# Attention probabilities transposed by a DMA through DRAM instead of on TensorE (top-k attention followed by a gated feed-forward block)

## The chip, the cores and the metric

The kernel runs on one core of a Trainium2 chip. The metric is device time in microseconds (us), the median of several runs. Profiles are taken of one execution each; their own time is given beside their span.

## The reference

The inputs q, k and v have the shape (batch 8, heads 8, sequence 576, head width 64); the weights are w_in (512 x 2048) and w_out (2048 x 512). All arithmetic is in float32.

```python
scores = (q @ k.T) / 8                      # per batch and head, 576 x 576
kth    = 32nd largest of each row
scores = where(scores >= kth, scores, -1e9)
attn   = softmax(scores)                    # divided by (sum + 1e-9)
x      = (attn @ v), heads side by side     # 4608 tokens x 512
h      = x @ w_in                           # 4608 x 2048
out    = (h * cos(h)) @ w_out               # 4608 x 512
```

## The kernel before

**Units.** The attention work is cut into 144 units: 128 rows of queries times one pair of heads. One unit's scores are a tile `s` of 128 partitions x 2 heads x 576 keys. The main loop has one iteration, called a slot here, per unit. It is written out by hand, and each engine carries out its instructions in the order in which the loop issues them. In slot i four units are in work: `u` (unit i) has its 32 largest scores per row found on VectorE; `w` (unit i-1) is masked and exponentiated on ScalarE, gets its reciprocal on VectorE and is normalised on GpSimd; `x` (unit i-2) is transposed; `y` (unit i-3) is multiplied with v on TensorE. The scores of unit i+1 are also made in slot i.

**What each engine is given in a slot, in order.**
- VectorE (DVE): four rounds of `topk_round(u, 0..3)` (two `max` and two `match_replace` in each, the last round only the two `max`). `reciprocal(w)` (a `tensor_scalar` on `den`, then the reciprocal) stands between round 2 and round 3; it waits for ScalarE's exponentials of w.
- ScalarE (ACT): evictions of feed-forward results (`take_banks`), `take_values(y)`, `take_scores` of unit i+1, then `mask(w)` and `exponentials(w)`, which need the bounds of w, then `take_transposes(x)` (three copies out of PSUM) and the sines of the feed-forward part.
- GpSimd (POOL): `bounds(w)` (two tiny instructions that need the last round of w), `gate` (one product of 128 x 1024), `reduce_first` and `reduce_second` (three `tensor_scalar` and one `tensor_tensor` of 128 x 1024 for the range reduction of the cosine, in those slots that have a finished tile of h), then `normalise(w)` (two `tensor_scalar` of 128 x 576).
- TensorE (PE): `values(y)`, the scores of unit i+1, two feed-forward units, `transposes(x)` (nine transposes of 128 x 128 against an identity), and the remaining feed-forward units.
- SyncE (SP) issues all DMAs in program order: loads of q, k, v and of the weights, and stores of the output.

**The feed-forward part** is fed into the gaps of TensorE in units of eight matmuls of 128 x 256 on the profile's count (`ff1`, first product) or four of 128 x 512 (`ff2`, second product), 288 of each. A credit of 3.7 units per slot, capped at 5, limits the feeding. What is left when the units run out is done by a loop at the end, in which VectorE takes over the work that GpSimd had.

**The first eight units** (`EARLY`) are treated differently, because the weights are decoded at that time on ScalarE, VectorE and GpSimd: for them the transposition, the product with v and its eviction all lie in the same slot as the exponentials, and GpSimd has `normalise(w)` before the decoding (`decode_third`, pairs of `tensor_tensor`) and before `reduce_first` and `reduce_second`.

PSUM has a tile with the tag `sc` in one copy, used by the scores and by the transposes in turn, and one with the tag `ot`, used by the values and by the last transpose.

Of the kernel before, what the change touches and what calls it, by code (L numbers as in the profile page):

```python
# [10 lines left out]
F32 = mybir.dt.float32  # L11
I32 = mybir.dt.int32
U32 = mybir.dt.uint32
AF = mybir.ActivationFunctionType
ALU = mybir.AluOpType

P = 128
# [13 lines left out]
def kernel(  # L31
# [9 lines left out]
    nc = tc.nc  # L41
    ctx.enter_context(tc.manual_schedule())
    B, H, D, S = qT.shape
    DM, DF = moe_w_in.shape
    NT = S // P
    TAIL = S - NT * P
    MAIN = NT * P
# [9 lines left out]
    work = ctx.enter_context(tc.tile_pool(name="work", bufs=2))  # L57
    small = ctx.enter_context(tc.tile_pool(name="small", bufs=4))
    ps = ctx.enter_context(tc.tile_pool(name="ps", bufs=2, space=bass.MemoryType.PSUM))
    ffw = ctx.enter_context(tc.tile_pool(name="ffw", bufs=2))  # L60

    ident = consts.tile([P, P], F32, tag="ident")
# [10 lines left out]
    words = 2 if DECODE else 1  # L73
# [7 lines left out]
    for i in range(DF // CW):  # L81
        w = consts.tile([P, NC, CW], F32, tag=f"w_in{i}", name=f"w_in{i}")
# [4 lines left out]
    for f in range(NF):  # L87
        w = consts.tile([P, DM], F32, tag=f"w_out{f}", name=f"w_out{f}")
# [3 lines left out]
    ff = {"live": 0, "tick": 0, "now": 0, "credit": 0.0, "end": False, "kind": 0}  # L92
# [21 lines left out]
    def decode_first(n):  # L114


        for _ in range(min(n, len(wq["loaded"]))):
            st, w = wq["loaded"].popleft()
            lo, hi = st[:, :, 0], st[:, :, 1]
            nc.scalar.activation(out=w, in_=hi.bitcast(F32), func=AF.Abs, scale=2.0**16)  # L120
            nc.scalar.sign(hi.bitcast(F32), hi)
            nc.scalar.mul(out=lo, in_=lo.bitcast(U32), mul=2.0**-29)
            wq["second"].append((st, w))
# [79 lines left out]
                    )  # L203

    def take_scores(u):
        s = u["s"] = work.tile([P, 2, S], F32, tag="s", name="s", bufs=4)
        nc.scalar.copy(  # L207
            out=s.rearrange("p j (h w) -> p (j h) w", h=2),
            in_=u.pop("sc").rearrange("p j h w -> p (j h) w")[:, :, 0:HS],
        )  # L210

    def topk_round(u, rnd):
        s = u["s"]
        if rnd == 0:
            u["m8"] = small.tile([P, 2, TOPK], F32, tag="m8", name="m8")
            u["rest"] = work.tile([P, 2, S], F32, tag="rest", name="rest", bufs=1)
        m8, rest = u["m8"], u["rest"]
        src = s if rnd == 0 else rest
        at = slice(8 * rnd, 8 * rnd + 8)
        for j in range(2):  # L220
            nc.vector.max(m8[:, j, at], src[:, j])  # L221
        if rnd < TOPK // 8 - 1:
            for j in range(2):
                nc.vector.match_replace(rest[:, j], m8[:, j, at], src[:, j], NEG)  # L224
        else:
            del u["rest"]
# [12 lines left out]
    def mask(u):  # L239

        s, nb = u["s"], u.pop("nb")
        for j in range(2):
            nc.scalar.activation(  # L243
                out=s[:, j], in_=s[:, j], func=AF.Prelu, bias=nb[:, j, 1:2], scale=SCALE, alpha=FAR
            )

    def exponentials(u):
        s, nd = u["s"], u.pop("nd")
        den = u["den"] = small.tile([P, 2], F32, tag="den", name="den")
        for j in range(2):  # L250
            nc.scalar.activation(  # L251
                out=s[:, j], in_=s[:, j], func=AF.Exp, bias=nd[:, j : j + 1], scale=1.0,
                accum_out=den[:, j : j + 1],
            )

    def reciprocal(u):
        den = u.pop("den")
        nc.vector.tensor_scalar(out=den, in0=den, scalar1=EPS, scalar2=None, op0=ALU.add)
        u["rden"] = small.tile([P, 2], F32, tag="rden", name="rden")
        nc.vector.reciprocal(u["rden"], den)  # L260

    def normalise(u):
        s, rden = u["s"], u.pop("rden")
        for j in range(2):
            nc.gpsimd.tensor_scalar(  # L265
                out=s[:, j], in0=s[:, j], scalar1=rden[:, j : j + 1], scalar2=1.0,
                op0=ALU.mult, op1=ALU.mult,
            )

    def transposes(u):  # L270

        s = u.pop("s")
        tp = u["tp"] = ps.tile([P, 2, 2, 512], F32, tag="sc", name="tp", bufs=1)
        for j in range(2):
            for c in range(NT):
                k0 = j * TAIL + c * P
                nc.tensor.transpose(  # L277
                    tp[:, 0, j, c * P : (c + 1) * P], s[:, j, k0 : k0 + P], ident
                )
        tt = u["tt"] = ps.tile([P, 512], F32, tag="ot", name="tt", bufs=1)  # L280
        nc.tensor.transpose(
            tt[:, 0:P], s.rearrange("p j k -> p (j k)")[:, MAIN : MAIN + P], ident
        )

    def take_transposes(u):
        tp, tt = u.pop("tp"), u.pop("tt")
        pT = u["pT"] = work.tile([P, 2, NT * P], F32, tag="pT", name="pT")
        for j in range(2):
            nc.scalar.copy(out=pT[:, j], in_=tp[:, 0, j])  # L289
        pt = u["pT_tail"] = work.tile([P, P], F32, tag="pT_tail", name="pT_tail")  # L290
        nc.scalar.copy(out=pt, in_=tt[:, 0:P])  # L291

    def values(u):

        pT, pt = u.pop("pT"), u.pop("pT_tail")
        o = u["o"] = ps.tile([P, 512], F32, tag="ot", name="o", bufs=1)
        for b, _, rows, r0 in u["parts"]:
            st = pairs[b, u["hp"]]
            r = slice(r0, r0 + rows)
            for c in range(NT + 1):  # L300
                for j in range(2):
                    d = slice(j * D, (j + 1) * D)
                    if c < NT:
                        lhsT, rhs = st["v"][:, c, d], pT[:, j, c * P + r0 : c * P + r0 + rows]
                    else:
                        lhsT, rhs = st["v_tail"][:, d], pt[:, r]
                    nc.tensor.matmul(o[d, r], lhsT, rhs, start=c == 0, stop=c == NT)  # L307

    def take_values(u):
# [95 lines left out]
    def sines(least):  # L405
# [4 lines left out]
        for _ in range(n):  # L410
            blk, g, x, _, scale = waiting.popleft()
            nc.scalar.activation(out=x, in_=x, func=AF.Sin, bias=halfpi, scale=scale)  # L412
            sined.append((blk, g, x))

    def gate(n):
        for _ in range(min(n, len(sined))):
            blk, g, x = sined.popleft()
            eng = nc.vector if ff["end"] else nc.gpsimd
            eng.tensor_tensor(out=g, in0=g, in1=x, op=ALU.mult)  # L419
            blk["gated"].append(ff["tick"])  # L420
# [42 lines left out]
    def feed(n):  # L463

        ff["tick"] += 1
        while n > 0 and ff["credit"] >= 1:
            for kind in (ff["kind"], 1 - ff["kind"]):
                if (can_first, can_second)[kind]():
                    break
            else:  # L470
                return
            if kind == 0:
                ff1(*first.popleft())
            else:
                ff2(*second.popleft())
            ff["kind"] = 1 - kind
            n, ff["credit"] = n - 1, ff["credit"] - 1
# [30 lines left out]
    for i in range(NU + 3):  # L508
        ff["end"] = i >= NU
        u, w, x, y = (units[i - n] if 0 <= i - n < NU else None for n in range(4))  # L510
        early = w and i - 1 < EARLY
        if x and i - 2 < EARLY:
            x = None
        if y and i - 3 < EARLY:
            y = None
        ff["credit"] = min(ff["credit"] + 3.7, 5.0)
        ff["now"] += 1
        wq["ready"] = wq["done"]
        if w:
            bounds(w)  # L520
        if u:
            if i > 0:
                decode_second()
            topk_round(u, 0)
        take_banks()
        if y:
            values(y)
        if i + 1 < NU:
            scores(units[i + 1])
        if y:  # L530
            take_values(y)
        if i + 1 < NU:
            take_scores(units[i + 1])
        for load, b, hp in at_slot.get(i, []):
            load(b, hp)
        gate(1)
        if w:
            mask(w)
            exponentials(w)
        if early:  # L540
            reciprocal(w)
            normalise(w)
        if u:
            topk_round(u, 1)
            topk_round(u, 2)
        if w and not early:
            reciprocal(w)
        feed(2)
        take_banks()
        if i > 0:  # L550
            decode_third()
            decode_first(3)
        load_weights(3)
        reduce_first()
        if x:
            transposes(x)
            take_transposes(x)
        feed(4)
        if early:
            transposes(w)  # L560
            take_transposes(w)
            values(w)
            take_values(w)
        reduce_second()
        if w and not early:
            normalise(w)
        if u:
            topk_round(u, 3)
        sines(2)
# [47 lines left out]
```

## Time and profile before

| | |
|---|---|
| median of 3 runs | 1696.09 us (1695.43 to 1697.95) |
| the profiled execution | 1698.95 us, its span 1697.0 us |
| PE busy | 1559.6 us (92%) |
| DVE busy | 1523.7 us (90%) |
| ACT busy | 1165.5 us (69%) |
| POOL busy | 844.8 us (50%) |
| DMA queue of the loads and stores | 54.54 MB, 10.4% of 16 engines |
| transposes on PE (L277, L281) | 1296 matmuls, 197.1 us busy, overlapping |
| their evictions on ACT (L289, L291) | 432 copies, 193.2 us busy, overlapping |

Busy times of one engine overlap, since instructions are pipelined; where the time of a piece of work counts, the distance from its start to the start of what follows is the better measure. "L277" is line 277 of the kernel before. An entry "A <- B" among the waits says that A stood idle until B was done. The line numbers of the changed kernel are shifted: by 2 up to `normalise` and by some 15 after the new functions.

### The profile page before, as it was taken

Reading aid. Unit: us, or ns where it says so; the run is one execution under the profiler, and the core shown is the slowest. Engines: PE = TensorE matmul, PEld = TensorE weight load, DVE = VectorE, ACT = ScalarE, POOL = GpSimd, SP = SyncE. Lnnn points to the kernel's source line nnn. Section 1 sums busy time; section 2 is a strip of 40 time slices with the busy share of each in tenths; the row PEclk is TensorE's granted clock in tenths of the full one; section 3 lists DMA queues with packets and bytes.
Section 4 is the critical chain, followed back from the end, with each engine's and each line's share of the span. In section 5 each row is a group of like instructions: output and inputs, shape, how many; then the busy total and the mean of one; then the engine's idle time right before and its main releaser. Section 6 shows DMA issues by size and latency. Waiting matters only on the chain.

```text
span 1697.0 us, 26520 instructions
## 1 busy us (share of the span) xinstructions
PE 1559.6 (92%) x9616; PEld 1074.2 (63%) x9616; DVE 1523.7 (90%) x3261; ACT 1165.5 (69%) x2046; POOL 844.8 (50%) x968
## 2 busy tenths in 40 slices
PE   4556799797989999999999999999999999999998
PEld 2454577484766666666666666666666676666674
DVE  7999999999999999999999999999999999995220
ACT  6677567667576777777777777877777777776110
POOL 3678645455365555555545555555555554552000
PEclk9677899999999999999999999999999999999999
DMA  7332011001100021002000020011000110000000
GB/s 232 100 96 75 7 49 36 20 1 49 42 8 7 7 64 35 7 10 64 26 7 7 21 58 26 7 35 49 21 7 7 47 30 7 7 8 7 13 7 19
DMA packets 44227, 56.24 MB, mean 33 GB/s; under 512 B 10816, under 2 KB 27200, under 8 KB 44096
## 3 DMA queue, kind: packets, MB, share of 16 engines
q1 hardware_dynamic: 44096, 54.54, 10.4%
q8 instruction: 76, 1.25, 0.3%
q14 instruction: 55, 0.45, 0.1%
HBM read 45.09 MB, written 9.44 MB: 32 GB/s over the span
## 4 chain that ended last, share of the span: by engine, by line
PE 59%; ACT 16%; POOL 11%; DVE 11%; issue 2%; DMA 1%; SPq 0%; POOLq 0%; ACTq 0%
PE o L431 20%; PE mm L355 19%; PE o L307 8%; PE sc L197 8%; DVE m L221 5%; ACT s L251 5%; DVE rest L224 4%; PE tp L277 4%; ACT s L243 3%; POOL x L402 3%; ACT s L207 2%; POOL s L265 2%; ACT L251 2%; ACT pT L289 1%; POOL x L393 1%
## 5 line engine op out<-in xcount | busy, mean ns | idle before, releaser
L221 DVE MAX8 m<-rest 128x8 f32<-128x576 f32 x864 | 608.1, 746 | 0.0
L431 PE MATMUL o<-w_out,g 128*128 128x512 f32 x1152 | 548.5, 603 | 10.1 <-POOL g L419 7.0
L355 PE MATMUL mm<-xT,w_in 128*128 128x256 f32 (+1 forms) x2688 | 552.7, 353 | 0.3 <-ACT g L367 0.3
L355 PEld LDWEIGHTS mm<-xT,w_in 128*128 128x128 f32 x2688 | 446.9, 191 | 128.4 <-issue 89.8
L265 POOL TENSOR_SCALAR s<-s,rden 128x576 f32<-128x576 f32 x288 | 213.4, 753 | 441.6 <-DVE rden L260 289.5
L224 DVE MATCH_REPLACE8 rest<-m,rest 128x576 f32<-128x576 f32 x576 | 423.5, 743 | 0.0
L431 PEld LDWEIGHTS o<-w_out,g 128*128 128x128 f32 x1152 | 208.4, 191 | 197.5 <-issue 175.9
L207 ACT COPY s<-sc 128x1152 f32<-128x1152 f32 x144 | 161.2, 1120 | 127.4 <-PE sc L197 127.2
L243 ACT ACTIVATE s<-s,nb 128x576 f32<-128x576 f32 x288 | 207.6, 770 | 49.5 <-POOL nb L231 49.5
L251 ACT ACTIVATE s<-s,nd 128x576 f32<-128x576 f32 x288 | 219.9, 765 | 0.7
L307 PE MATMUL o<-pT,v 128*64 128x128 f32 (+1 forms) x2560 | 168.5, 277 | 55.8 <-ACT pT_tail L291 55.7
L307 PEld LDWEIGHTS o<-pT,v 128*64 128x64 f32 x2560 | 133.3, 142 | 133.9 <-ACT pT_tail L291 90.0
L224 DVE MATCH_REPLACE8 rest<-m,s 128x576 f32<-128x576 f32 x288 | 211.7, 743 | 0.0
L221 DVE MAX8 m<-s 128x8 f32<-128x576 f32 x288 | 202.1, 743 | 8.0 <-ACT s L207 8.0
L277 PE MATMUL tp<-ident,s 128*128 128x128 f32 x1152 | 156.7, 281 | 55.7 <-POOL s L265 45.6
L197 PE MATMUL sc<-k,q 64*128 64x288 f32 (+1 forms) x1280 | 193.1, 449 | 11.6 <-DMA k<-in_k_dram 11.6
L277 PEld LDWEIGHTS tp<-ident,s 128*128 128x128 f32 x1152 | 138.2, 145 | 102.3 <-POOL s L265 52.6
L393 POOL TENSOR_SCALAR x<-g 128x1024 f32<-128x1024 f32 x63 | 66.2, 1050 | 205.8 <-ACT g L367 205.8
L289 ACT COPY pT<-tp 128x512 f32<-128x512 f32 x288 | 152.8, 582 | 17.4 <-PE tp L277 15.7
L314 ACT COPY xT<-o 128x128 f32<-128x128 f32 x144 | 37.9, 263 | 182.1 <-PE o L307 182.0
L419 POOL TENSOR_TENSOR g<-g,x 128x1024 f32<-128x1024 f32 x62 | 146.9, 2369 | 11.6 <-ACT x L412 11.6
L402 POOL TENSOR_TENSOR x<-g,x 128x1024 f32<-128x1024 f32 x63 | 149.3, 2370 | 5.3
(44 smaller groups left out, 1254.4 us busy)
## 6 DMA issues: line engine op xcount, KB each, us to landing
q<-in_q_dram SPq DMA_DIRECT2D x32, 288.0 KB, 3.1
out_dram<-ob SPq DMA_DIRECT2D x36, 256.0 KB, 2.0
st<-in_moe_w_in_dram SPq DMA_DIRECT2D x16, 512.0 KB, 5.1
v<-in_v_dram SPq DMA_DIRECT2D x32, 256.0 KB, 3.0
st<-in_moe_w_out_dram SPq DMA_DIRECT2D x16, 512.0 KB, 3.5
k<-in_k_dram SPq DMA_DIRECT2D x32, 144.0 KB, 3.3
k<-in_k_dram SPq DMA_DIRECT2D x32, 128.0 KB, 3.3
v_tail<-in_v_dram SPq DMA_DIRECT2D x64, 16.0 KB, 2.7
```

What stands on the lines that cost most here:

```text
L197: nc.tensor.matmul(sc[r0 : r0 + rows, j, h, 0:HS], st["q"][d, q0 : q0 + rows], st["k"][d, h * HS : (h + 1) * HS], start=True, stop=True,)
L207: nc.scalar.copy(out=s.rearrange("p j (h w) -> p (j h) w", h=2), in_=u.pop("sc").rearrange("p j h w -> p (j h) w")[:, :, 0:HS],)
L221: nc.vector.max(m8[:, j, at], src[:, j])
L224: nc.vector.match_replace(rest[:, j], m8[:, j, at], src[:, j], NEG)
L243: nc.scalar.activation(out=s[:, j], in_=s[:, j], func=AF.Prelu, bias=nb[:, j, 1:2], scale=SCALE, alpha=FAR)
L251: nc.scalar.activation(out=s[:, j], in_=s[:, j], func=AF.Exp, bias=nd[:, j : j + 1], scale=1.0, accum_out=den[:, j : j + 1],)
L265: nc.gpsimd.tensor_scalar(out=s[:, j], in0=s[:, j], scalar1=rden[:, j : j + 1], scalar2=1.0, op0=ALU.mult, op1=ALU.mult,)
L277: nc.tensor.transpose(tp[:, 0, j, c * P : (c + 1) * P], s[:, j, k0 : k0 + P], ident)
L307: nc.tensor.matmul(o[d, r], lhsT, rhs, start=c == 0, stop=c == NT)
L355: nc.tensor.matmul(mm[:, at : at + w], w_in[f // FC][:, c, (f % FC) * P : (f % FC + 1) * P], blk["xT"][:, c], start=c == 0, stop=c == NC - 1,)
L402: nc.gpsimd.tensor_tensor(out=x, in0=g, in1=x, op=ALU.subtract)
L431: nc.tensor.matmul(o, g[:, at : at + P], w_out[f], start=f == 0, stop=f == NF - 1)
```

## The change

For all units behind the first eight, the nine transposes on TensorE and the three copies out of PSUM are replaced. GpSimd copies the normalised probabilities once more, with the low and the high 16-bit halves of each float32 put into two separate rows (`split`, 2304 elements of 16 bits per partition). SyncE stores these rows to a DRAM tile (576 KB), and in the next slot a DMA of the transposing kind reads them back as 256 rows of 1152 16-bit columns and writes them to `pT`, which gives each float32 word its two halves side by side again. `values` reads `pT` as before, in the same slot as before.

To get there in time, `reciprocal(w)` moves from behind round 2 to behind round 1 on VectorE, and `normalise(w)` with `split(w)` follows it directly; on GpSimd this puts both ahead of `reduce_first` and `reduce_second`, where `normalise` stood behind them. The tile `s` has three copies instead of four, the tag `sc` is no longer shared with transposes behind the first eight units, and the credit goes from 3.7 to 4.0 feed-forward units per slot. The first eight units keep their transposes on TensorE (`transposes_now`).

```diff
+    dram = ctx.enter_context(tc.tile_pool(name="dram", bufs=4, space=bass.MemoryType.DRAM))
...
     def take_scores(u):
-        s = u["s"] = work.tile([P, 2, S], F32, tag="s", name="s", bufs=4)
+        s = u["s"] = work.tile([P, 2, S], F32, tag="s", name="s", bufs=3)
...
+    def split(u):
+        s = u.pop("s").rearrange("p j k -> p (j k)").bitcast(U16)
+        halves = work.tile([P, 2, 2 * S], U16, tag="halves", name="halves", bufs=1)
+        nc.gpsimd.tensor_copy(out=halves, in_=s.rearrange("p (k h) -> p h k", h=2))
+        rows = u["rows"] = dram.tile([P, 2, 2 * S], U16, tag="rows", name="rows")
+        nc.sync.dma_start(out=rows, in_=halves)
+
     def transposes(u):
+        rows = u.pop("rows").rearrange("q h k -> (q h) k")
+        pT = u["pT"] = work.tile([P, 2 * NT + 1, P], F32, tag="pT", name="pT")
+        words = pT.rearrange("p c q -> p (c q)").bitcast(U16)
+        nc.sync.dma_start_transpose(
+            out=words.rearrange("p (c q) -> p c q", c=2 * NT + 1), in_=rows
+        )
-        s = u.pop("s")
-        tp = u["tp"] = ps.tile([P, 2, 2, 512], F32, tag="sc", name="tp", bufs=1)
...
-    def take_transposes(u):
...
-            nc.scalar.copy(out=pT[:, j], in_=tp[:, 0, j])
...
-        ff["credit"] = min(ff["credit"] + 3.7, 5.0)
+        ff["credit"] = min(ff["credit"] + 4.0, 5.0)
...
         for load, b, hp in at_slot.get(i, []):
             load(b, hp)
+        if x:
+            transposes(x)
         gate(1)
...
             topk_round(u, 1)
-            topk_round(u, 2)
         if w and not early:
             reciprocal(w)
+            normalise(w)
+            split(w)
+        if u:
+            topk_round(u, 2)
         feed(2)
...
         reduce_first()
-        if x:
-            transposes(x)
-            take_transposes(x)
         feed(4)
         if early:
-            transposes(w)
-            take_transposes(w)
+            transposes_now(w)
             values(w)
             take_values(w)
         reduce_second()
-        if w and not early:
-            normalise(w)
         if u:
             topk_round(u, 3)
```

## The prediction, made before the changed kernel had run

> **What bounds the kernel now.** I read the busy times by slice first, then busy times in windows, then the engines' timelines. From 600 us to 1550 us two engines are full at once:
>
> ```profile
> core 0: us, PE busy (x) PEld busy (x) DVE busy (x) ACT busy (x) POOL busy (x), PEclk, DMA share, GB/s
> 1200.00:1300.00 100.00, 98.07 (x574) 67.11 (x570) 98.73 (x219) 76.86 (x136) 54.98 (x64) 1.00 0.04 12
> 1550.00:1600.00 50.00, 50.00 (x210) 33.35 (x209) 11.94 (x12) 13.31 (x19) 0.76 (x1) 1.00 0.02 6
> ```
>
> In the first row PE and DVE are both above 98%; in the second, after the last unit, PE works off feed-forward units alone. The DVE timeline gives the length of a slot:
>
> ```profile
> 810.34 0.50 DVE L258 TENSOR_SCALAR den<-den 128x2 f32<-128x2 f32 x1
> ...
> 820.59 0.16 DVE L258 TENSOR_SCALAR den<-den 128x2 f32<-128x2 f32 x1
> ```
>
> The `den` before stood at 800.30, so slots last 10.04 and 10.25 us; I use 10.0. DVE needs that by itself: a `max` or `match_replace` follows the other after 0.66 us, 14 of them with their value loads are 9.6 us, the reciprocal 0.3. PE's order in one slot, from the chain that ended last:
>
> ```profile
> 815.35 1.92 PE mm L355 x8
> 817.27 1.72 PE o L431 x4
> 818.99 0.87 PE tp L277 x8
> 819.86 0.11 PE tt L281
> 819.97 1.73 PE mm L355 x8
> 821.70 1.72 PE o L431 x4
> 823.42 1.24 PE o L307 x20
> ```
>
> The transposes take 0.87 + 0.11 = 0.98 us, the values 1.24, scores 1.17, a feed-forward unit 1.73. With 3.7 units that is 9.8 us and a little for changes of kind. The place that will decide is the first stage, where GpSimd already has work between a normalise and the next bounds:
>
> ```profile
> 116.27 0.20 POOL L231 TENSOR_SCALAR nb<-m 128x4 f32<-128x4 f32 x1
> 116.55 0.19 POOL L236 TENSOR_TENSOR nd<-nb 128x2 f32<-128x2 f32 x1
> 120.07 1.47 POOL L265 TENSOR_SCALAR s<-s,rden 128x576 f32<-128x576 f32 x2 [3.32 <-ACT g L367]
> 121.50 1.29 POOL L139 TENSOR_TENSOR w_out<-w_out,st 128x512 int32<-128x512 int32 x1
> ...
> 139.41 1.47 POOL L265 TENSOR_SCALAR s<-s,rden 128x576 f32<-128x576 f32 x2 [3.31 <-ACT w_out L120]
> ```
>
> ```profile
> 119.49 0.17 DVE L258 TENSOR_SCALAR den<-den 128x2 f32<-128x2 f32 x1 [2.63 <-ACT s L251]
> ```
>
> Bounds at 116.27, next normalise at 120.07: 3.8 us in which POOL waits for mask, exponentials and reciprocal. Then 1.43 for the normalise, 8.1 for decoding, 6.0 for the range reduction, 3.8 again: 19.3 us, exactly the distance between the two normalises. It is a ring (normalise, POOL's other work, bounds, exponentials, reciprocal, normalise), and it is longer than DVE's own work, so DVE stands 2.63 us at `den`. Later this ring is harmless, because the reduction lies between bounds and normalise, beside ScalarE's part.
>
> **The change, part by part.**
>
> *PE and the credit.* 0.98 us per slot goes. At 4.0 units PE has 1.24 + 1.17 + 4 x 1.73 + about 0.2 = 9.5 us, below DVE's 10.0, so PE alone allows the slot to stay at 10.0. By the two programs' instruction order 89 feed-forward units follow the last scores before, 57 after: 32 x 1.73 = 55 us less tail. That is the whole gain, since DVE's work is unchanged. The removed evictions (about 1.3 us of ACT per slot) free an engine that is 77% busy and off the path: nothing by itself. Cover: were PE the later one, each 0.1 us per slot would cost 14 us over 136 slots.
>
> *Order on GpSimd.* Normalise and split now precede the range reduction, so the reduction lies between them and the next slot's bounds: the ring of the first stage is back in each slot with a reduction. Its length: bounds to normalise 3.8, normalise 1.43, split C, reduction 5.76 (in the timeline the four instructions start at 805.06 and end at 810.82). That is 11.0 + C, against 10.0. ScalarE waits for the bounds behind this, DVE waits at `den` behind ScalarE, and DVE cannot catch up, since its own work fills a slot. Without a reduction the ring is 5.2 + C, shorter than a slot.
>
> *C.* No copy of 16-bit elements is in the trace. Nearest are POOL's one-input rows: L393, 1024 elements in 1050 ns, gives 2304 / 1024 x 1.05 = 2.4 us; the two rows of L265 and L393 together give a slope of 0.66 ns per element, so 1.7 at least; at the two-input rate (L402, 2370 ns for 1024) it would be 5.3. I take 2.4, since it has one input.
>
> So a slot with a reduction lasts 13.4 us, 3.4 longer. In the instruction order 65 of the 136 late units' slots have one: 65 x 3.4 = +220 us. In 16 of these a sine precedes, so that the exponentials reload their table (L251, 1.28 us) inside the ring: +20.
>
> *The transfers.* Another ring goes over two slots: reciprocal, normalise 1.67, split C, store R, transposing read T, values 1.24, scores 1.17 behind them on PE, `take_scores` 1.14, then mask and exponentials 2.96 on ACT and the reciprocal 0.74: 9.0 + C + R + T, with 0.1 for the issue. Values, scores and `take_scores` stand ahead of the mask, so a late transpose stops ScalarE and with it DVE.
>
> ```profile
> out_dram<-ob SPq DMA_DIRECT2D x36, 256.0 KB, 2.0
> ...
> v<-in_v_dram SPq DMA_DIRECT2D x32, 256.0 KB, 3.0
> st<-in_moe_w_out_dram SPq DMA_DIRECT2D x16, 512.0 KB, 3.5
> ...
> v_tail<-in_v_dram SPq DMA_DIRECT2D x64, 16.0 KB, 2.7
> ```
>
> R, 576 KB to DRAM: between 3.4 (2.0 plus 320 KB more at the first slice's 232 GB/s) and 4.5 (2.0 x 576/256); I take 3.5, the `st` row. T is not in the trace. Its source is 2304 pieces of 256 bytes. Between v_tail (64 pieces, 2.7) and v (512 pieces, 3.0) a piece costs 0.7 ns, which gives 4.2 us. The queue's total (10.4% of 16 engines over 1697 us for 44096 packets) is 64 ns a packet, on one of 16 engines 9.2, plus 2.7: 11.9. I take 6, nearer to the bulk rows, because `st` lands in 3.5 with 512 KB. The ring is then 20.9 us over two slots. Two slots with one reduction take 23.4 and cover it; the 23 pairs without one take 20.0: 23 x 0.9 = +21.
>
> The Trainium skill has two rules on T that contradict each other. "VectorE: DVE Perf Modes", section "The three transpose paths", puts a 128 x 128 transpose of 16 bits by DMA at 1309 ns against 390 on TensorE, which speaks against the change. An estimate from that figure is 18 blocks one after another, 23.6 us, a slot of 19.3 us and a total near 2900 us. "Advanced Engine Details and Errata", section "X-Bar Transpose (TRN2)", calls such DMAs as fast as ordinary ones, which would make T about the 4 us of the `st` row and leave out the 21. No run so far shows which holds.
>
> *Queues.* SP now waits in order for split, and for the store before each transposing read; behind it stand loads of q, k and v, made a slot or more ahead, and output stores. I cost this at nothing; if loads came late they would show as PE waiting for k (11.6 us in all before). *Three copies of s:* `take_scores` must wait for the split two units back, a ring of 6.5 + C = 8.9 us, below 10; at C = 5.3 it would be 11.8. *PE's clock* may be granted a little less at 80% busy (0.97 where PE was 86% busy, 300 to 400 us); PE has room for that.
>
> *Sum,* on the profiled execution: 1698.95 - 55 + 220 + 20 + 21 = 1905 us. The median lay 2.9 below that execution, so 1902.
>
> **Rivals.**
>
> *The transfers set the slot.* At T = 11.9 the ring of the transfers is 9.0 + 2.4 + 3.5 + 11.9 = 26.8, 13.4 per slot, in all slots: 136 x 3.4 = 462, so 1698.95 - 55 + 462 - 3 = about 2103. For it: small pieces, and packets at 64 ns. Against: SP's DMAs are 10% busy. The mark is PE waiting for a DMA at the values.
>
> *The copy is slow.* C = 5.3: slots with a reduction 16.3 (65 x 6.3 = 410), the others 11.8 (71 x 1.8 = 128), with the 20: about 2199. The mark is the copy's own duration.
>
> *Faster.* The reduction does not stop DVE, because the next bounds are not late where it matters. Then only the shorter tail is left: 1696 - 55 = 1641. The price of a reduction slot is C + 1.0, and 65 of them outweigh 55 us from 0.85 us each; so even at C = 0 (65 us) it would not be faster. It needs the reductions to run elsewhere, for instance waiting for ScalarE's g in the slot's second half and covered by slots of DVE. Against: the first stage shows the ring adding up to 0.1 us. At a break-even in between nothing would change.
>
> **How the numbers follow.** The ring over POOL with a quick copy and T up to about 8: 0.62, predicted 1902. Transfers decisive: 0.2. Slow copy: 0.12. Faster 0.05, no change 0.01; 0.2% is about what a measurement here can tell. The lower end is C = 1.7 without the cost of the transfers: 1902 - 21 - 65 x 0.7 = 1835, and I go to 1825 for the tail. The upper end takes in the transfers' case at 2103 and part of the slow copy's: 2170. Left out are the faster cases, and transfers beyond 13 us.
>
> **What would show it.** `den` waiting for ScalarE (about 260 us in all, 38.5 before), in slots of 13.4 and 10.0 us by turns; POOL without a pause from normalise over split and reduction to bounds; PE about 80% busy; the tail after the last `max` near 97 us (153 before, from 1543.75). The prediction is wrong if DVE still stays at 98%, if PE waits mostly for `pT` from a DMA, or if the copy is not near 2.4 us.

## The result and the profile after

The changed kernel takes 1906.26 us (median of 4 runs, 1905.05 to 1909.26), the kernel before 1697.02 us beside it: a ratio of 1.1234, with a 95% interval from 1.1215 to 1.1254. The prediction was 1902 us, slower with a chance of 0.94.

The profiled execution has a span of 1904.0 us against 1697.0. The busy times by window, in the same columns as before:

```profile
core 0: us, PE busy (x) PEld busy (x) DVE busy (x) ACT busy (x) POOL busy (x), PEclk, DMA share, GB/s
1200.00:1300.00 100.00, 85.07 (x465) 54.39 (x464) 82.27 (x183) 53.85 (x88) 64.94 (x64) 0.93 0.37 103
1800.00:1904.00 104.00, 92.50 (x450) 57.73 (x448) 22.71 (x29) 22.79 (x36) 12.70 (x12) 0.97 0.14 40
```

In the first row no engine is full: DVE was at 98.7 us of 100 and is at 82.3, PE went from 98.1 to 85.1. That all five engines are partly idle fits a ring of waits, each engine waiting for the next. The stage behind the last `max`, called the tail here, is shorter: that `max` ends at 1808.05 instead of 1543.75, and 95.9 us follow it, where 153.2 did.

POOL's timeline shows the ring over one slot with a reduction and into the next:

```profile
1013.96 1.46 POOL L267 TENSOR_SCALAR s<-s,rden 128x576 f32<-128x576 f32 x2 [3.65 <-DVE rden L262]
1015.49 2.10 POOL L279 COPY halves<-s 128x2304 uint16<-128x2304 uint16 x1
1017.56 1.05 POOL L408 TENSOR_SCALAR x<-g 128x1024 f32<-128x1024 f32 x1
...
1020.95 2.36 POOL L417 TENSOR_TENSOR x<-g,x 128x1024 f32<-128x1024 f32 x1
1023.27 0.21 POOL L233 TENSOR_SCALAR nb<-m 128x4 f32<-128x4 f32 x1
1023.56 0.19 POOL L238 TENSOR_TENSOR nd<-nb 128x2 f32<-128x2 f32 x1
1023.71 2.35 POOL L434 TENSOR_TENSOR g<-g,x 128x1024 f32<-128x1024 f32 x1
1027.05 1.47 POOL L267 TENSOR_SCALAR s<-s,rden 128x576 f32<-128x576 f32 x2 [0.99 <-ACT g L382]
```

From normalise to normalise: 1027.05 - 1013.96 = 13.09 us. POOL has no pause from the normalise over the copy and the reduction to the bounds at 1023.27; from there to the next normalise it is 3.8 us. DVE stands at `den` meanwhile, and is free of it in the slot without a reduction that follows:

```profile
1026.50 0.17 DVE L260 TENSOR_SCALAR den<-den 128x2 f32<-128x2 f32 x1 [3.08 <-ACT s L253]
1036.42 0.16 DVE L260 TENSOR_SCALAR den<-den 128x2 f32<-128x2 f32 x1
```

The waits (engine, line, releaser: us in total, times, longest):

```profile
DVE den L260 <- ACT s L253: 307.8, 111, 5.8
...
PE o L446 <- ACT ob L455: 143.2, 29, 5.9
...
PE o L446 <- POOL g L434: 81.2, 21, 11.3
...
PE o L322 <- DMA pT<-rows: 54.3, 29, 9.7
```

The first was 38.5 us before:

```profile
DVE den L258 <- ACT s L251: 38.5, 33, 3.5
```

PE's waits for `ob` and for the gates' `g` were 3.0 and 7.0 us before. The transfers do not carry the loss: PE waits 54.3 us for `pT`, 39 of them before 600 us. The new operations themselves, from the page and from the answers on `halves` and `pT`:

```profile
rows<-halves SPq DMA_DIRECT2D x136, 576.0 KB, 2.8
```

```profile
L279 POOL COPY halves<-s x136: 2102/2102/2971, 159.3 to 1814.7; 128x2304 uint16<-128x2304 uint16 x136
```

```profile
L287 SPq DMA_TRANSPOSE pT<-rows x136: 2170/2544/4312, 167.4 to 1820.7; - x136
...
DMA to landing us min/median/max: 4.4/4.6/6.5
```

The copy takes 2.10 us, the store 2.8. The transposing read is 4.6 us from its issue to landing, and SP's queue is occupied by its issue for 2.54 us of that (0.34 for the store).

### The profile page after: what moved, and what is told of

Its sections match the earlier page's. It is cut to its first block, busy times and chain, and to the rows that moved or that the text cites. A ratio compares the mean times of both kernels' runs of the same rounds, so it can differ in the third digit from the quotient of the medians.

```text
span 1904.0 us, 24525 instructions
## 1 busy us (share of the span) xinstructions
PE 1524.3 (80%) x8392; PEld 984.6 (52%) x8392; DVE 1505.9 (79%) x3249; ACT 987.7 (52%) x1622; POOL 1161.5 (61%) x1124
## 4 chain that ended last, share of the span: by engine, by line
PE 33%; POOL 32%; ACT 23%; issue 6%; DVE 3%; DMA 2%; SPq 0%; POOLq 0%; ACTq 0%; DVEq 0%
PE o L446 12%; PE mm L370 12%; POOL halves L279 8%; ACT s L253 7%; POOL x L417 7%; ACT s L245 5%; PE o L322 5%; PE sc L199 4%; POOL s L267 3%; ACT s L209 3%; POOL x L409 3%; POOL x L410 3%; POOL x L408 3%; POOL g L434 2%; ACT L253 2%
## 5 line engine op out<-in xcount | busy, mean ns | idle before, releaser
L446 PE MATMUL o<-w_out,g 128*128 128x512 f32 x1152 | 621.7, 677 | 235.3 <-ACT ob L455 143.2
L370 PEld LDWEIGHTS mm<-xT,w_in 128*128 128x128 f32 x2688 | 462.1, 194 | 146.7 <-issue 96.3
L446 PEld LDWEIGHTS o<-w_out,g 128*128 128x128 f32 x1152 | 232.9, 215 | 514.0 <-issue 316.0
L279 POOL COPY halves<-s 128x2304 uint16<-128x2304 uint16 x136 | 286.8, 2109 | 8.6
L260 DVE TENSOR_SCALAR den<-den 128x2 f32<-128x2 f32 x144 | 24.1, 167 | 308.2 <-ACT s L253 307.8
L322 PE MATMUL o<-pT,v 128*64 128x128 f32 (+1 forms) x2560 | 174.2, 282 | 84.8 <-DMA pT<-rows 54.3
L322 PEld LDWEIGHTS o<-pT,v 128*64 128x64 f32 x2560 | 139.2, 145 | 152.4 <-issue 56.6
L382 ACT ACTIVATE g<-mm 128x512 f32<-128x512 f32 x144 | 84.3, 586 | 164.9 <-PE mm L370 163.4
L417 POOL TENSOR_TENSOR x<-g,x 128x1024 f32<-128x1024 f32 x67 | 158.0, 2358 | 5.6
L434 POOL TENSOR_TENSOR g<-g,x 128x1024 f32<-128x1024 f32 x66 | 155.7, 2360 | 1.1 <-ACT x L427 0.9
L199 PEld LDWEIGHTS sc<-k,q 64*128 64x128 f32 (+1 forms) x1280 | 106.4, 191 | 58.1 <-issue 20.0
```

The costliest lines, as they stand in the source:

```text
L199: nc.tensor.matmul(sc[r0 : r0 + rows, j, h, 0:HS], st["q"][d, q0 : q0 + rows], st["k"][d, h * HS : (h + 1) * HS], start=True, stop=True,)
L279: nc.gpsimd.tensor_copy(out=halves, in_=s.rearrange("p (k h) -> p h k", h=2))
L370: nc.tensor.matmul(mm[:, at : at + w], w_in[f // FC][:, c, (f % FC) * P : (f % FC + 1) * P], blk["xT"][:, c], start=c == 0, stop=c == NC - 1,)
L417: nc.gpsimd.tensor_tensor(out=x, in0=g, in1=x, op=ALU.subtract)
L446: nc.tensor.matmul(o, g[:, at : at + P], w_out[f], start=f == 0, stop=f == NF - 1)
```

## The experiments

Slots are counted from one reciprocal to the next; all but the first, which belong to the early units, are sorted into those with a reduction and those without (65 and 69 in the changed kernel).

**1. The reduction ahead of the normalise.** The DMAs, the copy and the early reciprocal stay; the order on POOL becomes that of before.

```diff
         gate(1)
+        late = w and not early
+        if late:
+            reduce_first()
+            reduce_second()
...
-        reduce_first()
+        if not late:
+            reduce_first()
```

> The range reduction is issued between bounds and normalise again, beside ScalarE's part, all else as in the changed kernel. Theory (the reduction lies in the ring of normalise, split, reduction, bounds, exponentials, reciprocal): no slot has a ring of 13.1 us any more. The 41 late slots with a reduction alone hold 0.5 + 5.8 + 1.5 + 2.1 = 9.9 us of GpSimd work, the 24 with a gate as well 12.2; so about 1906 - 65 x 2.7 + 24 x 1.5 = 1766 us, and VectorE's wait at den falls from 308 us to below 170. Rival (the store and the transposing read set the slots): nothing changes, 1906.

Measured: 1731.52 us, ratio 1.0207 (1.0192 to 1.0222).

```profile
DVE den L260 <- ACT s L253: 89.5, 70, 4.6
```

DVE waits 89.5 us at `den`, where it waited 307.8; slots with a reduction have a median of 10.6 us where they had 13.08. Moving these four instructions takes back 175 of the 209 us: DMA, copy and traffic are all still there. It is better than the theory's 1766, which had charged the remaining slots more. Of what is left, a part is of another kind: the addition on `den` itself, 165 ns in the changed kernel, takes over 400 ns in 52 of 144 cases here, 39 us longer in all, a matter that experiment 11 takes up.

**2. The order alone.** The kernel before, transposes on TensorE, with only the reciprocal behind round 1 and the normalise ahead of the reduction.

```diff
             topk_round(u, 1)
-            topk_round(u, 2)
         if w and not early:
             reciprocal(w)
+            normalise(w)
+        if u:
+            topk_round(u, 2)
...
-        if w and not early:
-            normalise(w)
```

> The kernel before, with its transposes on TensorE, its credit of 3.7 and its four copies of s, and only the reciprocal moved behind round 1 and the normalise put ahead of the range reduction: the order of the change without its copy and its DMAs. Theory: slots with a reduction get a ring of 11.0 us (12.3 with a table load) against 10.4 before, so 1697 + 61 x 0.6 to 1697 + 61 x 1.5, some 1735 to 1790 us. Rival (only the transfers cost): 1697.

Measured: 1816.08 us, ratio 1.0707 (1.0691 to 1.0723). No DMA has been added, and 119 us are lost. POOL's timeline has the same ring without the copy, here with a table load in it:

```profile
926.70 1.47 POOL L265 TENSOR_SCALAR s<-s,rden 128x576 f32<-128x576 f32 x2 [5.45 <-DVE rden L260]
928.14 1.04 POOL L393 TENSOR_SCALAR x<-g 128x1024 f32<-128x1024 f32 x1
...
933.86 0.20 POOL L231 TENSOR_SCALAR nb<-m 128x4 f32<-128x4 f32 x1
...
939.08 1.47 POOL L265 TENSOR_SCALAR s<-s,rden 128x576 f32<-128x576 f32 x2 [2.42 <-DVE rden L260]
```

That is 12.38 us (12.3 were expected); without a table load the median is 10.95 (11.0). The total lies 26 us above the theory's range. The slots with a reduction, 42 of the 61 with the table load inside the ring, lost about 107 us, where at most 92 had been allowed, and the slots without one lost some 13, where none had been. The rival, that the order costs nothing by itself, is out.

**3. An eighth of the copy.**

```diff
-        nc.gpsimd.tensor_copy(out=halves, in_=s.rearrange("p (k h) -> p h k", h=2))
+        few = 2 * S // 8
+        nc.gpsimd.tensor_copy(
+            out=halves[:, :, 0:few], in_=s.rearrange("p (k h) -> p h k", h=2)[:, :, 0:few]
+        )
```

> Only the first eighth of each row's halves is copied on GpSimd, into a tile that is kept and was zeroed at the start (the rest of the probabilities is left out); store and transposing read have their full size. Theory: slots with a reduction shrink by the whole of the saved copy, some 1.8 us, from 13.1 to 11.3 (14.5 to 12.7 with a table load), slots without one stay where they are, 10 to 11.4: 65 x 1.8 less, about 1790 us. Rival (the transfers' ring over two slots): both kinds of slot shrink alike, by 0.9 each.

Measured: 1801.61 us, ratio 1.0619 (1.0603 to 1.0635). The copy falls from 2102 to 423 ns, the slots with a reduction and no table load from a median of 13.08 to 11.29 us: in their ring the copy counts with its full length. The total fell by 105 us: 84 of them in the 65 slots with a reduction, 1.29 each on average, and 22 in the 69 others, 0.3 each. So the two kinds did not shrink alike, as the rival had it, but the slots without a reduction did not stay where they were either; why they became shorter was not tried.

**4. The transposing read twice.**

```diff
-        nc.sync.dma_start_transpose(
-            out=words.rearrange("p (c q) -> p c q", c=2 * NT + 1), in_=rows
-        )
+        for _ in range(2):
+            nc.sync.dma_start_transpose(
+                out=words.rearrange("p (c q) -> p c q", c=2 * NT + 1), in_=rows
+            )
```

> The changed kernel with each transposing read made twice, one after the other, into the same tile. Rival (the transfers set the slots): the read, 4.6 us from issue to landing and 2.5 us of issue alone, gets 2.5 to 4.6 longer, over two slots: 136 x 1.3 to 136 x 2.3, so 2080 to 2220 us. Theory (the ring over GpSimd): the transfers' ring is 9.0 + 2.1 + 2.8 + 4.6 = 18.5 us over two slots and becomes 21 to 23; only the 23 pairs of slots without a reduction (20 to 21 us) feel it, so 1906 to 1965 us.

Measured: 2114.28 us, ratio 1.2461 (1.2431 to 1.249). My theory's range is missed, the rival's is met. Here the transfers are the bound, in the chain that ended last and in the waits:

```profile
DMA 36%; PE 28%; POOL 14%; ACT 12%; issue 4%; SPq 4%; DVE 2%; ACTq 0%; POOLq 0%
```

```profile
PE o L323 <- DMA pT<-rows: 319.0, 98, 12.2
```

SP's timeline shows one reason why a pair of reads of 9.4 us weighs more than its length:

```profile
1002.91 7.71 SPq L288 DMA_TRANSPOSE pT<-rows  x2
1010.72 0.53 SPq L281 DMA_DIRECT2D rows<-halves  x1
1014.81 0.40 SPq L182 DMA_DIRECT2D v<-in_v_dram  x1
1015.25 1.15 SPq L187 DMA_DIRECT2D v_tail<-in_v_dram  x2
1016.50 7.25 SPq L288 DMA_TRANSPOSE pT<-rows  x2
```

Read, values on PE, the load of v that waits for those values, and the next read behind it in SP's order: a ring of one slot, 13.6 us from read to read here. A load of q waits for PE's scores in the same way (SP stands 140.1 us for these in all, 52.8 for the loads of v). The 27 slots with a load of q last 15.5 us on average and the 27 with one of v 13.9, where the 80 with neither last 13.1; with one read all three kinds are at 12.1 to 12.3. So some two thirds of the loss lies in the slots with a load, and the rest is in the others. The prediction had costed SP's order at nothing: that holds with one read, and not with two.

**5. The reciprocal late again.** Reciprocal, normalise and split of the changed kernel stand behind round 2.

```diff
             topk_round(u, 1)
+            topk_round(u, 2)
         if w and not early:
             reciprocal(w)
             normalise(w)
             split(w)
-        if u:
-            topk_round(u, 2)
```

> The changed kernel with reciprocal, normalise and split behind round 2 again, 2.8 us later on VectorE. Theory: the ring of the reduction has no part of VectorE's rounds in it, so slots with a reduction stay at 13.1 us (14.5 with a table load); slots without one but with a table load fall from 11.4 to about 10, since ScalarE has 8.3 us in place of 5.5 between bounds and den: 31 x 1.4 = 45 us less, about 1860. Rival (the transfers set the slots): the transfers start later, so it gets slower, up to 1906 + 136 x 1.4.

Measured: 1910.22 us, ratio 1.1256 (1.1238 to 1.1275): no gain. The slots with a reduction stayed at 13.08 us, as expected. My expectation for the others fell: they are not long because `den` comes early, since 47 of the 69 stayed the same to 0.05 us (slots 105, 113, 121: 12.66, 12.67, 12.67 us; in the changed kernel 12.66, 12.66, 12.67) and their mean did not fall. The rival, that later transfers would cost up to 190 us, fell too. What is seen of these slots stands behind experiment 7.

**6. The reduction in two parts.** The window between bounds and normalise takes three of the four instructions of the reduction, or a gate; the fourth, or another gate, stands behind the split.

```diff
-        gate(1)
+        late = w and not early
+        if late and fresh and len(fresh[0]) < 3 and len(waiting) + len(sined) < XB:
+            reduce_first()
+        elif late and not sined:
+            reduce_second()
+        else:
+            gate(1)
```

> The changed kernel with GpSimd's feed-forward work dealt out in parts: between bounds and normalise either the first three instructions of the reduction (3.4 us) or a gate, behind the split the fourth (2.4 us) or a gate. Theory: the longest ring is 3.8 + 1.5 + 2.1 + 2.4 = 9.8 us without a table load and 11.1 with one, so slots of 10 to 11 and 1680 to 1720 us, less than the 1731 of the kernel that has the whole reduction ahead of the normalise. Rival (GpSimd's sum of work counts, not its place): as there, 1731.

Measured: 1769.28 us, ratio 1.0424 (1.0407 to 1.0441). A miss: slots with a reduction came out as expected (medians 10.1 and 11.1 with a table load), but the slots without one grew to a mean of 11.2. The likely reason is that gates behind the split are late and the second product on PE waits for their `g`; no run tried this by itself. (A slot counts as one with a reduction here if it has its fourth instruction.)

**7. No change of ScalarE's function table.**

```diff
-            nc.scalar.activation(out=x, in_=x, func=AF.Sin, bias=halfpi, scale=scale)
+            nc.scalar.activation(out=x, in_=x, func=AF.Prelu, bias=halfpi, scale=scale, alpha=1.0)
```

> The changed kernel with one word changed: the sine is replaced by the leaky-linear function (Prelu, slope 1) that the mask uses too, so that ScalarE never changes its function table between mask, exponentials and sines; the cosine is thereby left out of the result, all else is done as before. Theory (the slots with a sine but no reduction, 31 of them at 11.44 us, are long because two table loads of 1.28 us use up the slack that ScalarE has between the scores and the time at which den waits): these slots fall to 10.0 to 10.3 us, the 16 slots with both a sine and a reduction from 14.5 to about 13.1, the others stay: 1906 - 31 x 1.3 - 16 x 1.4 = about 1843 us (1830 to 1860), den wait about 245 us. Rival (the sines themselves and the evictions around them, or the feed-forward units that wait for gates, make these slots long): they stay at 11 us or more, only the 16 fall: 1880 us or more.

Measured: 1868.63 us, ratio 1.1008 (1.0992 to 1.1024): 38 us less, halfway between the two expectations. The 65 slots with a reduction lost 25 us, as the theory had it; the others only 13 of their 61 us over 10.0. So the table loads explain about a fifth of these 61 us, and the rest is elsewhere.

One way of it is seen in the changed kernel's own timelines, PE, ACT and POOL in turn, over two slots without a reduction (reciprocals at 1440.5, 1450.4 and 1463.1):

```profile
1438.33 5.20 PE L446 MATMUL o<-w_out,g 128*128 128x512 f32 x8 [2.49 <-POOL g L434]
1443.46 1.09 PE L322 MATMUL o<-pT,v 128*64 128x128 f32 x16
...
1445.87 8.90 PE L370 MATMUL mm<-xT,w_in 128*128 128x256 f32 x40
1454.70 1.09 PE L322 MATMUL o<-pT,v 128*64 128x128 f32 x16
1455.63 0.39 PE L322 MATMUL o<-pT,v_tail 128*64 128x128 f32 x4
1455.94 1.24 PE L199 MATMUL sc<-k,q 64*128 64x288 f32 x8
```

```profile
1457.29 1.12 ACT L209 COPY s<-sc 128x1152 f32<-128x1152 f32 x1 [0.96 <-PE sc L199]
1458.30 1.44 ACT L245 ACTIVATE s<-s,nb 128x576 f32<-128x576 f32 x2
```

```profile
1454.89 0.19 POOL L238 TENSOR_TENSOR nd<-nb 128x2 f32<-128x2 f32 x1
```

The bounds are done at 1455.08, but the mask starts at 1458.30, directly behind `take_scores`. PE had stood 2.49 us for a gate that POOL ran late, a unit was put off, and the next slot did five units in 8.90 us before the values. In 46 of the 69 slots without a reduction the mask starts over 0.6 us behind its bounds; these last 11.37 us on average, the others 9.93. In 18 of the 69 PE does five or more units without a pause: 11.93 us, 35 of the 61 us.

**8. No unit saved up.**

```diff
-        ff["credit"] = min(ff["credit"] + 4.0, 5.0)
+        ff["credit"] = min(ff["credit"] + 4.0, 4.0)
```

> The changed kernel with the credit capped at 4.0 instead of 5.0, so that no slot can catch up on a feed-forward unit that an earlier slot did not find ready. In the changed kernel 46 of the 69 slots without a reduction have the mask standing more than 0.6 us behind its bounds, directly behind take_scores; 18 of these slots follow five units on TensorE without a pause and are 11.9 us long (35 us over 10.0). Theory (in these slots TensorE's chain of units, values, scores, take_scores, mask, exponentials sets the end): without the fifth unit they fall to 10.0 to 10.9 us, slots without a reduction have a mean of about 10.5 instead of 10.89, that is 25 to 30 us less up to the last max; the 20 to 30 units not caught up on are done at the end, 35 to 50 us more tail; 1905 to 1930 us in all. Rival (ScalarE's function tables and sines alone set these slots): their mean stays near 10.9, the last max stays at 1808 us, and the total rises by the whole tail to 1940 or more.

Measured: 1975.83 us, ratio 1.1638 (1.1618 to 1.1657): a miss. The five-unit slots did go, but the rhythm of gates and sines shifted: 36 slots with a reduction have a table load in the ring (16 in the changed kernel), and in 69 slots PE pauses over 1 us between one unit's scores and the next values (53). Slots without a reduction have a mean of 11.49 us. That long slots go with a late mask is seen more sharply (42 slots at 12.44 us, the others 10.01); that the fifth unit costs 35 us by itself is not shown.

**9. The credit alone.** The kernel before with 4.0 in place of 3.7.

> The kernel before with one number changed: a credit of 4.0 feed-forward units per slot in place of 3.7; the transposes stay on TensorE. Theory (the shorter tail is worth something only because the transposes have left PE): PE then needs 0.98 + 1.24 + 1.17 + 4 x 1.73 + 0.2 = 10.5 us per slot, 0.3 to 0.5 above the slots of before, so 136 slots lose 40 to 65 us while the tail behind the last max loses about 50: 1685 to 1715 us, PE near 98% in the slots, tail about 100 us. Rival (the credit alone brings the gain, PE has room for it): slots stay near 10.2 us, tail about 100 us, total about 1645 us.

Measured: 1742.59 us, ratio 1.0271 (1.0253 to 1.0288). The tail is 97 us, but the last `max` ends 99.5 us later than before, more than the 40 to 65 expected. At a credit of 4.0 and with the transposes on PE, the shorter tail costs more than it brings; no run shows why the loss is larger than PE's busy time says.

**10. The ring cut.** The copy, store and read as in the changed kernel, but the normalise and the split run one slot later, behind that slot's bounds; read and values move one slot as well, and mask and exponentials stand ahead of `take_values` and `take_scores` on ACT.

```diff
-    for i in range(NU + 3):
+    for i in range(NU + 4):
...
-        u, w, x, y = (units[i - n] if 0 <= i - n < NU else None for n in range(4))
+        u, w, x, t, y = (units[i - n] if 0 <= i - n < NU else None for n in range(5))
...
+        if w:
+            mask(w)
+            exponentials(w)
...
-        if x:
-            transposes(x)
+        if t:
+            transposes(t)
         gate(1)
-        if w:
-            mask(w)
-            exponentials(w)
+        if x:
+            normalise(x)
+            split(x)
...
             topk_round(u, 1)
+            topk_round(u, 2)
         if w and not early:
             reciprocal(w)
-            normalise(w)
-            split(w)
-        if u:
-            topk_round(u, 2)
```

> The ring is cut: reciprocal behind round 2, normalise and split one slot later, behind that slot's bounds; the transposing read and the values one slot later too; on ScalarE mask and exponentials stand ahead of take_values and take_scores. Normalise, split, transfers, values and scores then lie in no ring with bounds, exponentials and reciprocal; GpSimd has 12.2 us of work in a slot with gate and reduction and 8.1 on average. Theory: slots of 10.0 us as before the change, with the shorter tail of 96 us and one slot more of latency at the end: 1640 to 1670 us, faster than both. Rival (the copy, the DMAs or contention cost VectorE time of their own): slots stay above 10.5 and it is not below 1697.

Measured: 1658.49 us, ratio 0.9766 (0.9749 to 0.9782): faster than both kernels, as expected. The chain that ended last and POOL's timeline:

```profile
DVE 81%; PE 11%; POOL 4%; issue 1%; ACT 1%; DMA 1%; SPq 0%; DVEq 0%; POOLq 0%; ACTq 0%
```

```profile
1012.82 0.20 POOL L233 TENSOR_SCALAR nb<-m 128x4 f32<-128x4 f32 x1 [3.54 <-DVE m L223]
1013.11 0.19 POOL L238 TENSOR_TENSOR nd<-nb 128x2 f32<-128x2 f32 x1
1013.27 1.47 POOL L267 TENSOR_SCALAR s<-s,rden 128x576 f32<-128x576 f32 x2
1014.80 2.10 POOL L279 COPY halves<-s 128x2304 uint16<-128x2304 uint16 x1
```

POOL now waits for DVE's last `max`, and the normalise follows the bounds with no wait for a reciprocal. The median slot is 9.98 us, `den` waits 13.8 us in all. Against before, the last `max` ends 11.6 us later (1555.4) and the tail is 50.5 shorter (102.7). The slots without a reduction, whose mask no longer stands behind `take_scores`, have a mean of 9.98 us (10.89 in the changed kernel), which fits what is seen behind experiment 7. Several edits were made at once, the loads of v one slot later among them; what each is worth was not tried.

**11. Without the addition to the sums.** In the kernel of experiment 10 some `den` instructions were long, and the page's chain put 3% on them:

```profile
998.90 2.27 DVE L260 TENSOR_SCALAR den<-den 128x2 f32<-128x2 f32 x1
```

```profile
998.79 2.35 POOL L417 TENSOR_TENSOR x<-g,x 128x1024 f32<-128x1024 f32 x1
```

```diff
         den = u.pop("den")
-        nc.vector.tensor_scalar(out=den, in0=den, scalar1=EPS, scalar2=None, op0=ALU.add)
```

> The kernel of the run with the bounds ahead of the normalise, with the addition of 1e-9 to the sums on VectorE left out (the reciprocal takes the sums directly; each sum is at least 1, so the addition does not change a float32). In that kernel the addition, 165 ns by itself, took more than 400 ns in 56 of 144 cases and ended 22 to 28 ns behind a GpSimd instruction that ran beside it, up to 2.27 us; this sums to 43.6 us, all on VectorE, which sets the slot there. Theory (the addition waits for GpSimd's instruction to end, the reciprocal, 165 ns everywhere, does not): the 43.6 us go, and 0.25 us per slot for the addition itself, less what TensorE's chain then holds back: slots of 9.75 to 9.9 us, 1658 - 44 - (0 to 30) = 1585 to 1625 us. Rival (whatever VectorE issues in that place waits, or the delay is covered by another wait): the reciprocal becomes the long one or the mask comes late, and the time stays at 1645 to 1660 us.

Measured: 1607.49 us, ratio 0.9478 (0.946 to 0.9497), inside the theory's range. Slots have a median of 9.70 us, and PE and DVE are full again:

```profile
1200.00:1300.00 100.00, 97.20 (x528) 61.58 (x527) 99.40 (x217) 65.92 (x107) 77.50 (x75) 1.00 0.48 131
```

**12. The same without DMA transposes.** The same line taken out of the kernel before.

> The kernel before (transposes on TensorE) with the same addition of 1e-9 left out: a control for the run without the addition, which took 1607 us. In the kernel before 25 of the 144 additions were long, 15.3 us in all. Theory (before, TensorE is nearly as full as VectorE, so a shorter VectorE slot is taken up by TensorE's chain): 5 to 30 us less, 1665 to 1690 us, TensorE above 98% in the slots; the larger gain needs the transposes off TensorE. Rival (the addition alone is what the faster kernel gained, the transposes have nothing to do with it): 1697 - 15 - 34 = 1650 us or less.

Measured: 1694.98 us, ratio 0.998 (0.997 to 0.9989): less than the 5 to 30 us expected, and far from the rival. So the 5% of experiment 11 is not the addition's by itself: with the same line gone it is 1607.5 us there against 1695.0 here. What it needs is something of experiment 10, that is the transposes off TensorE, the credit of 4.0 or the new order; these were not tried one by one.

## Why the prediction was right

**The ring over POOL** was the cause, and its sizes were right. Predicted 11.0 + C per slot with a reduction; measured 13.08, and C is 2.10 (2.4 was taken), so the 11.0 holds to 0.02 us in the median. 65 slots had a reduction, 16 of them a table load as well (14.50 us), as counted. Their excess over 10.0 us is 235 us (163 + 72); predicted 220 + 20. That these sums agree so closely is in part luck: the copy, taken 0.3 us too long, made 65 slots 20 us too dear, and some of these slots lasted longer than their ring by 12 us in all. The floor of 1.7 us for the copy was misread: the line through the two rows named reaches 1.9 us at 2304 elements. Experiment 1 shows the cause, 2 shows it without the DMAs, 3 prices the copy in it.

**The tail**: 57.3 us shorter, predicted 55. Experiment 9 adds that with the transposes left on PE the same tail costs 99.5 us ahead of it.

**The transfers**: the store was 2.8 us (3.5 taken), the read 4.6 (6 taken). By the prediction's sum the ring over two slots is then 9.0 + 2.1 + 2.8 + 4.6 = 18.5 us, below the 20.0 of two quick slots: the 21 us charged to it were not there. Of the two rules that the Trainium skill has on the read, "Advanced Engine Details and Errata", section "X-Bar Transpose (TRN2)", came nearer, though the read is not as fast: 4.6 us against 2.8 for the plain store of the same size, and 3.3 and 5.0 for the `st` rows of w_out and w_in (512 KB). The 1309 ns that "VectorE: DVE Perf Modes", section "The three transpose paths", gives are for one block of 128 x 128, which no run here reads by itself; the estimate of 18 such blocks one after another is not borne out, since 18 blocks in 4.6 us are 0.26 us a block.

**The step that failed**, inside a total that came out right, is the one on slots without a reduction: "Without a reduction the ring is 5.2 + C, shorter than a slot", with "PE alone allows the slot to stay at 10.0". Both hold, yet these 69 slots have 61 us over 10.0, where the 21 us of the transfers stood. PE's 9.5 us is a mean; its order is feed-forward units, values, scores, and behind them on ACT `take_scores` and mask. A wait of PE for a gate or for `ob` (81.2 and 143.2 us in all, 7.0 and 3.0 before), or a fifth unit after it, can reach `den` by that way, as the timeline behind experiment 7 shows once. Experiment 5 shows that the reciprocal's place does not matter to these slots, 7 that the table loads are about a fifth of it; the sizes of the rest are read from the timeline, and experiment 8 did not separate them.

**The sum** agreed better than its terms. Against 10.0 us per slot the changed kernel has 235 + 61 = 296 us; the kernel before has 30, which the prediction had set to nothing. The difference, 266, is about the later last `max` (+264.3); predicted 261. Three misses of -5, +40 and -30 cancelled: that the total came within 5 us is luck, the mechanism and the size of its largest term are not.

**The marks**: `den` waited 307.8 us for ScalarE (about 260 named), PE is 80% busy, the tail is 95.9 (97), and PE waits 8.5 us for k (11.6 before), so the loads behind SP's new waits did not come late. The slots without a reduction are not all 10.0.

**The rivals.** Transfers did not set the slot, but a read of twice the length did (experiment 4). The copy was not slow. The faster outcome was ruled out in this order of work, and experiments 10 and 11 show that it was there in another.

## What to carry to other kernels

On engines that work in order, look first at which wait a moved instruction now stands ahead of: here four instructions of 5.8 us on an engine that is 61% busy cost 175 us by their place, while 136 round trips through DRAM left the median slot at 9.98 us (9.91 before) once they were off the ring. Give long work a place behind the last thing that the next engine waits for, and pay with one more slot of depth. Cost the slots by class, not by a mean, since an in-order engine hands on each of its waits.

## What the runs showed of the hardware

- A tiny VectorE addition (128 x 2, 165 ns alone) beside a GpSimd instruction can last until 20 to 29 ns after that instruction's end: over 400 ns in 56 of 144 cases in experiment 10, 43.6 us in all, 25 and 15.3 us in the kernel before, none in the changed kernel, where DVE reached it while POOL waited. The reciprocal never did: at most 168 ns in these three kernels, and 179 in experiment 11, where it stands in the same place. The Trainium skill, "SBUF — State Buffer", section "Who interferes with whom", describes a port pair that the two engines share by an exclusive lock; the rows agree with it.
- The issue of a transposing read of 576 KB keeps SP's queue for 2.5 us, the plain store of the same size for 0.34; from the end of the issue to landing it is 2.07 us more in the median.
- DMA traffic did not slow VectorE's `max`: in experiment 10, at 136 GB/s and 48% of the DMA engines between 1200 and 1300 us, a `max` takes 745 ns in the median (743 over the whole kernel), against 743 in the kernel before.
- The granted TensorE clock is a mean of 0.90 in the changed kernel, 0.97 before, though PE is less busy (80% against 92%). Between 1200 and 1300 us it is 0.93, against 1.00 before and 1.00 in experiment 11. What the lower clock costs by itself no run shows.
